# Rounding every second quad of an FFN's activations by a casting transfer instead of on VectorE

## The chip, the cores and the metric

The kernel runs on one core of a Trainium2 chip. The metric is the device time of one launch in microseconds (us); lower is better. The kernel before took 1745.02 us in the median of 3 runs (1744.55 to 1746.68).

The engines are written as the profile writes them: PE (TensorE, matrix products; PEld its weight loads), DVE (VectorE), ACT (ScalarE), POOL (GpSimd) and SP (SyncE, which issues the transfers of the kernel before).

## The reference

Four sequences of 12480 tokens with 128 channels go through an induced attention (32 learned points attend to the tokens, then the tokens attend to the result), and every token then through a feed-forward net with a squared ReLU.

```python
I = np.broadcast_to(inducing[None], (B, m, C))        # B, N, m, C = 4, 12480, 32, 128
def mab(q, kv):
    s = scale * (q @ kv.transpose(0, 2, 1))
    a = np.exp(s - s.max(-1, keepdims=True))
    a /= a.sum(-1, keepdims=True) + 1e-09
    return a @ kv
h = mab(I, x)
attn = mab(x, h)                                      # (4, 12480, 128)
h = np.maximum(attn.reshape(B * N, C) @ w_in, 0.0)    # w_in (128, 2048)
out = (h * h @ w_out)                                 # w_out (2048, 128)
```

## The kernel before

**Tiles.** The tokens are cut into 52 units of 960 tokens, 13 to a sequence (a batch). A unit has two blocks of 480 tokens. The 2048 hidden columns are 16 f-tiles of 128, and four f-tiles make a quad, so a block has four quads, j = 0 to 3.

**One quad.** PE forms h for four f-tiles (line 782), two to each of two PSUM tiles. ACT writes their ReLU into a tile g of 128 x 1920 (line 790, two instructions), then squares g in place (line 801). DVE writes hi, which is g rounded to the narrower format in which PE multiplies in one pass (line 805), and lo = g - hi (line 809). PE then adds twelve products to the block's output op in PSUM (line 822): hi with the high part of w_out, hi with its low part, and lo with its high part, four each. So each number of g is read by ACT, by DVE twice and by PE, and hi and lo are what PE waits for.

**The attention.** What the tokens' second attention gives a block (st) is made a unit ahead in small steps on PE, DVE and ACT (the class Second), with the eviction sw written by ACT or DVE, whichever the planner finds free (line 235), and four transfers sw to st. Beside it a first pass over a later unit runs (the class First): a load xn, a load xq that DVE turns into xt, scores, exponentials, and sums. After the last unit of a batch has had its first pass, a short stage joins the sums; GpSimd's instruction sums belongs to it. First passes run 14 units ahead, so the last units of the program have none beside them.

**What sets the order.** Nothing is ordered by hand. Each step is a task with an engine, a duration, a due time, the tasks it needs and the buffers it takes; the class Plan lays the tasks out in time, greedily, and the instructions are then written on each engine in the order of the plan's starts. LATENCY is what Plan adds between a task of an engine and one that needs it. An engine works its instructions in that order: one that waits holds up all behind it on its engine. GB, HB and LB are the numbers of buffers for g, hi and lo, and `room` tells Plan of them.

**Names.** In the order rows below a name such as hi_8_0_3 is followed by a running number: unit 8, block 0, quad 3 (the batch is left out). In h_8_1_5 the last figure is one of a block's eight PSUM tiles, two to a quad, so h_8_1_4 and h_8_1_5 feed g_8_1_2.

Of the kernel before, what the change touches and what calls it, by code (L numbers as in the profile page):

```python
# [12 lines left out]
F32R = mybir.dt.float32r  # L13
# [8 lines left out]
TS = 120  # L22
# [22 lines left out]
class Plan:  # L45
# [2 lines left out]

    ENGINES = ("PE", "ACT", "DVE", "POOL", "SP")

    LATENCY = {"PE": 220.0, "ACT": 150.0, "DVE": 185.0, "POOL": 150.0, "SP": 2500.0}
    SWITCH = 95.0
    LATE = {"PE": 200.0, "other": 100.0}

# [4 lines left out]
    def add(self, engine, ns, fn, due, needs=(), port=False, mode=None, takes=(), reads=(), late=None):  # L61

        if late is None:
            late = self.LATE["PE" if engine == "PE" else "other"] if due > self.begin else 0.0
        needs = [n for n in needs if n is not None]
        t = Task(engine.split("|"), ns, fn, due, needs, port, mode, takes, late, len(self.tasks))  # L70
        for b in list(takes) + list(reads):
            b.users.append(t)
        self.tasks.append(t)
        return t

    def run(self):
        free = {e: 0.0 for e in self.ENGINES}
        mode = None
        port = 0.0
        taken = {}  # L80
        open_ = {e: [] for e in self.ENGINES}
        done = []

        def offer(t):
            t.ready = 0.0
            for n in t.needs:
                own = n.by == "PE" and t.engine == ["PE"]
                t.ready = max(t.ready, n.end + (0.0 if own else self.LATENCY[n.by] + t.late))
            for e in t.engine:
# [24 lines left out]
        while len(done) < len(self.tasks):  # L114
            best = None
            for e in self.ENGINES:
                pick = None
# [37 lines left out]
def induced_attention_then_squared_relu_ffn(  # L155
# [8 lines left out]
    nc = tc.nc  # L164
    B, N, C = x.shape
    M = inducing.shape[0]
# [3 lines left out]
    NU = N // UNIT  # L170
    Q = P // M
    scale = 1.0 / math.sqrt(C)
    NQ = NF // 4
    GB, HB, LB = 3, 2, 2
    PERIOD, START, T_MAIN, NARROW, STEP = 32000.0, 2600.0, 66000.0, 6000.0, 1700.0
    W_DUE = [8000.0 + 6500.0 * k for k in range(8)]

# [3 lines left out]

    const = ctx.enter_context(tc.tile_pool(name="const", bufs=1))
    xn_pool = ctx.enter_context(tc.tile_pool(name="xn", bufs=3))
    xq_pool = ctx.enter_context(tc.tile_pool(name="xq", bufs=2))
    xt_pool = ctx.enter_context(tc.tile_pool(name="xt", bufs=NU + 1))
    hw_pool = ctx.enter_context(tc.tile_pool(name="hw", bufs=2))
    att = ctx.enter_context(tc.tile_pool(name="att", bufs=2))
# [1 line left out]
    ps_h = ctx.enter_context(tc.tile_pool(name="ps_h", bufs=2, space=PSUM))  # L189
    ps_o = ctx.enter_context(tc.tile_pool(name="ps_o", bufs=2, space=PSUM))  # L190
    ps_m = ctx.enter_context(tc.tile_pool(name="ps_m", bufs=2, space=PSUM))
    plan = Plan(dict(xn=3, early=6, xt=NU + 1, m=2, h=2, o=2, g=GB, hi=HB, lo=LB, st=2, sw=2, rows=2, xq=2, words=2), T_MAIN)

    def bank(name):
        return ps_m.tile([P, 512], F32, tag="m", name=name)
# [35 lines left out]
    add = plan.add  # L231
# [385 lines left out]
    class Second:  # L617
# [14 lines left out]
        def weigh(self, scored, where, bank_, due, step):  # L632
            v = {}
            n, s, u = self.n, self.s, self.u
# [37 lines left out]
                nc.vector.tensor_mul(v["d"], v["d"], v["rz"].broadcast_to([TS, G, M]))  # L672

            def high():
                v["sk"] = att.tile([TS, Q, 2, 2, M], F32R, tag="sk", name=f"sk_{n}")
                nc.vector.tensor_copy(v["sk"][:, :, :, 0, :], v["d"].rearrange("t (k q) m -> t q k m", q=Q))

            def low():
# [39 lines left out]
            t = add("DVE", 115, invert, d + 3 * step, [t])  # L718
            t = add("DVE", 340, share, d + 4 * step, [t], port=True)
            th = add("DVE", 210, high, d + 4 * step, [t], port=True)  # L720
            tl = add("DVE", 335, low, d + 5 * step, [th], port=True)
            t = add("PE", 460, back, d + 5 * step, [tl], takes=[ba])
# [38 lines left out]
    def ffn_block(b, u, k, second, t0, first_needs):  # L761
        n = f"{b}_{u}_{k}"
        s = state[b]
        w = {}
        bo = Buffer("o")
        part = PERIOD / 2 / NQ
        last = None

        def quad(j, last):
            v = {}  # L770
            due = t0 + j * part
            bg, bhi, blo = Buffer("g"), Buffer("hi"), Buffer("lo")
            relus = []
            for i in range(2):
                bh = Buffer("h")
                c = {}

                def wide(l, i=i, c=c):
                    if l == 0:
                        c["hp"] = ps_h.tile([P, 2, 512], F32, tag="h", name=f"h_{n}_{2 * j + i}")  # L780
                    f = 4 * j + 2 * i + l
                    nc.tensor.matmul(  # L782
                        c["hp"][:, l, :BLK], s["hw"][:, f * P:(f + 1) * P], s["st", u][:, k, :],
                        start=True, stop=True,
                    )

                def relu(i=i, c=c):
                    if i == 0:
                        v["g"] = pools["ffn"].tile([P, 4, BLK], F32, tag="g", name=f"g_{n}_{j}", bufs=GB)
                    nc.scalar.activation(v["g"][:, 2 * i:2 * i + 2, :], c["hp"][:, :, :BLK], AF.Relu)  # L790

                d = due + i * part / 2
                need = [second.ready, s["wide"][j]]
                t = add("PE", 219, lambda wide=wide: wide(0), d, need, takes=[bh], reads=[second.bst], late=LATE_G1)
                w.setdefault("begun", t)
                t = add("PE", 219, lambda wide=wide: wide(1), d, [t], reads=[bh, second.bst])
                relus.append(add("ACT", 864, relu, d + 1000, [t] + first_needs + relus, late=0,
                                 takes=[bg] if i == 0 else [], reads=[bh] + ([bg] if i else [])))

            def square():  # L800
                nc.scalar.activation(v["g"], v["g"], AF.Square)  # L801

            def high():
                v["hi"] = pools["ffn"].tile([P, 4, BLK], F32R, tag="hi", name=f"hi_{n}_{j}", bufs=HB)
                nc.vector.tensor_copy(v["hi"], v["g"])  # L805

            def low():
                v["lo"] = pools["ffn"].tile([P, 4, BLK], F32R, tag="lo", name=f"lo_{n}_{j}", bufs=LB)
                nc.vector.tensor_sub(v["lo"], v["g"], v["hi"])  # L809

            sq = add("ACT", 1706, square, due + 4000, relus, reads=[bg], late=0)
            th = add("DVE", 1070, high, due + 5700, [sq], port=True, late=200, takes=[bhi], reads=[bg])
            tl = add("DVE", 2070, low, due + 7800, [th], port=True, late=0, takes=[blo], reads=[bg, bhi])
            for m, (wo, name, from_, buf) in enumerate((
                (wo_hi, "hi", th, bhi), (wo_lo, "hi", th, bhi), (wo_hi, "lo", tl, blo),
            )):
                for i in range(2):
                    def products(i=i, wo=wo, name=name, m=m):
                        if j == m == i == 0:
                            w["op"] = ps_o.tile([P, 512], F32, tag="o", name=f"op_{n}")  # L820
                        for l in (2 * i, 2 * i + 1):
                            nc.tensor.matmul(  # L822
                                w["op"][:, :BLK], wo[:, 4 * j + l, :], v[name][:, l, :],
                                start=(j == m == l == 0), stop=(j == NQ - 1 and m == 2 and l == 3),
                            )

                    begin = j == m == i == 0
                    last = add("PE", 438, products, due + 8000 + 600 * (2 * m + i), [from_, last, w_outs[j]],
                               takes=[bo] if begin else [], reads=[buf] + ([] if begin else [bo]))
            return last  # L830

        for j in range(NQ):
            last = quad(j, last)

        def rows():
            w["rows"] = att.tile([P, BLK // M, M], F32, tag="rows", name=f"rows_{n}")
            nc.vector.transpose(w["rows"].rearrange("p g c -> p (g c)"), w["op"][:, :BLK])  # L837

        def store():
            for q in range(Q):  # L840
                nc.sync.dma_start(out_v[b, u, k, q], w["rows"][q * M:(q + 1) * M])

        br = Buffer("rows")
        end = t0 + PERIOD / 2 + 8000
        t = add("DVE", 570, rows, end + 1500, [last], reads=[bo], late=LATE_OT, takes=[br])
        add("SP", 2000, store, end + 4000, [t], reads=[br])
        return w["begun"]
# [19 lines left out]
    for w, (b, u) in enumerate(units):  # L867
# [4 lines left out]
        f = g = None  # L872
        if a < len(units):
            f = firsts[a] = First(*units[a], t_u + NARROW)
        if a - 1 < len(units):
            g = firsts[a - 1]
# [43 lines left out]
```

## Time and profile before

| | us |
|---|---|
| median of 3 runs | 1745.02 |
| the profiled execution's own time | 1748.76 |
| its span, first to last instruction | 1746.8 |
| PE busy in the span | 1687.7 |
| DVE busy | 1665.2 |
| ACT busy | 1588.2 |
| POOL busy | 25.8 |
| DVE's 416 casts to hi | 477.6 |
| DVE's 416 subtractions to lo | 896.0 |

Two more facts of the page: the clock granted to PE is at full speed from about 112 us on (mean 0.987 over the span), and the DMA engines are busy 31.7% of the time, nearly all of it with short packets.

How to read the rows that follow. In a row of groups stand line, engine, operation, the tile written and the tiles read, their shapes, the count, then busy us and mean ns of one, then the idle time of the engine just before such instructions and what ended it. In a row of the timeline stand start and length in us, engine, line and operation, with the count if several are merged; brackets give the idle time before it and its releaser. In a row of the chain stand start, length and what ran. Busy time of PE has modelled ends and counts pipelined matmuls longer than the distance at which they follow each other.

### The profile page before, as it was taken

How to read it: one execution, taken by the hardware profiler on the slowest of the kernel's cores; microseconds unless marked ns; L12 is line 12 of the kernel's file. 1: busy time of each engine (PE TensorE's matmuls, PEld its weight loads, DVE VectorE, ACT ScalarE, POOL GpSimd, SP SyncE). 2: the span in 40 equal slices, each digit the busy share in tenths (PEclk: the TensorE clock that was granted, in tenths of full speed). 3: DMA queues.
4: the chain of work that ended last, by engine and by line, in shares of the span. 5: the costliest groups of instructions: out<-in, count | busy, mean ns of one | idle time of the engine just before them, and what ended most of it. 6: DMA issues, size and time to landing. Idle time of an engine off the chain costs nothing.

```text
span 1746.8 us, 23651 instructions
## 1 busy us (share of the span) xinstructions
PE 1687.7 (97%) x8897; PEld 1339.3 (77%) x8897; DVE 1665.2 (95%) x1777; ACT 1588.2 (91%) x1581; POOL 25.8 (1%) x22
## 2 busy tenths in 40 slices
PE   7699999999999999999999999999999999999998
PEld 4378777777877777777777877777787888888886
DVE  5689999999999999999999999999999999999998
ACT  5399999999989999999998999999998999999997
POOL 1200000000000000000000000000000000000000
PEclk9699999999999999999999999999999999999999
DMA  9742342333333333333423333423211121211111
GB/s 207 128 68 47 63 74 53 62 68 63 61 59 57 60 66 63 63 57 63 73 47 63 64 56 63 74 47 62 40 29 35 29 40 29 41 29 37 32 27 30
DMA packets 428781, 101.61 MB, mean 58 GB/s; under 512 B 362844, under 2 KB 428156, under 8 KB 428668
## 3 DMA queue, kind: packets, MB, share of 16 engines
q1 hardware_dynamic: 428668, 100.11, 31.7%
q8 instruction: 70, 1.15, 0.3%
q14 instruction: 43, 0.35, 0.1%
HBM read 48.94 MB, written 25.56 MB: 43 GB/s over the span
## 4 chain that ended last, share of the span: by engine, by line
PE 51%; DVE 30%; issue 11%; ACT 6%; DMA 2%; SPq 0%; DVEq 0%; POOL 0%; ACTq 0%
PE op L822 35%; PE h L782 12%; DVE lo L809 10%; DVE hi L805 10%; ACT g L801 3%; ACT g L790 2%; DVE rows L837 2%; DVE xt L401 1%; PE na L626 1%; DMA xn<-in_x_dram 1%; DVE sw L235 1%; DVE d L672 1%; DVE sk L680 1%; PE wp L586 1%; DMA words_o<-in_moe_w_out_dram 1%
## 5 line engine op out<-in xcount | busy, mean ns | idle before, releaser
L809 DVE TENSOR_TENSOR lo<-g,hi 128x1920 fp32r<-128x1920 f32 x416 | 896.0, 2154 | 16.2 <-PE na L430 0.5
L790 ACT ACTIVATE g<-h 128x960 f32<-128x960 f32 x832 | 783.0, 967 | 96.1 <-PE h L782 82.6
L801 ACT ACTIVATE g<-g 128x1920 f32<-128x1920 f32 x416 | 752.9, 1810 | 8.2
L782 PE MATMUL h<-st,hw 128*128 128x480 f32 x1664 | 517.9, 389 | 12.7 <-ACT g L790 8.2
L805 DVE CAST hi<-g 128x1920 fp32r<-128x1920 f32 x416 | 477.6, 1148 | 25.1 <-ACT g L801 19.7
L822 PE MATMUL op<-lo,wo_hi 128*128 128x480 f32 x1664 | 459.3, 390 | 15.2 <-DVE lo L809 15.1
L822 PE MATMUL op<-hi,wo_hi 128*128 128x480 f32 x1664 | 462.6, 386 | 1.3 <-DVE hi L805 1.0
L822 PE MATMUL op<-hi,wo_lo 128*128 128x480 f32 x1664 | 432.3, 382 | 0.0
L782 PEld LDWEIGHTS h<-st,hw 128*128 128x128 f32 x1664 | 308.7, 189 | 104.3 <-ACT g L790 54.3
L822 PEld LDWEIGHTS op<-lo,wo_hi 128*128 128x128 f32 x1664 | 297.4, 189 | 87.5 <-DVE lo L809 42.0
L822 PEld LDWEIGHTS op<-hi,wo_hi 128*128 128x128 f32 x1664 | 304.1, 188 | 68.7 <-DVE hi L805 20.2
L822 PEld LDWEIGHTS op<-hi,wo_lo 128*128 128x128 f32 x1664 | 313.8, 189 | 49.9
L837 DVE STREAM_TRANSPOSE rows<-op 128x480 f32<-128x480 f32 x104 | 70.4, 677 | 1.3 <-PE op L822 1.2
L401 DVE STREAM_TRANSPOSE xt<-xq 128x960 f32<-128x960 f32 x39 | 45.7, 1172 | 4.3 <-PE na L626 4.3
L687 PEld LDWEIGHTS ap<-identr,sk 120*128 120x128 f32 x208 | 31.4, 193 | 7.3 <-issue 4.0
L626 PE MATMUL na<-xt,hT 128*32 128x240 f32 x416 | 32.7, 387 | 0.0
L687 PE MATMUL ap<-identr,sk 120*128 120x120 f32 x208 | 29.5, 265 | 2.5 <-DVE sk L680 2.5
L235 ACT COPY xt<-xtp 128x480 f32<-128x480 f32 x26 | 14.3, 559 | 16.4 <-PE xtp L415 16.4
L564 POOL TENSOR_SCALAR sums<-ones,zs 128x128 f32<-128x128 f32 x4 | 8.8, 2209 | 1228.1 <-PE lp L548 800.0
L464 PE MATMUL ep<-ident,e 128*120 128x128 f32 x104 | 21.5, 290 | 5.0 <-ACT e L456 3.3
L415 PE MATMUL xtp<-ident,xn 120*128 120x120 f32 x104 | 18.6, 319 | 7.6 <-DMA xn<-in_x_dram 7.6
L430 PE MATMUL na<-xt,indT 128*32 128x240 f32 x312 | 23.8, 378 | 0.9 <-DVE xt L401 0.9
(90 smaller groups left out, 616.6 us busy)
## 6 DMA issues: line engine op xcount, KB each, us to landing
xn<-in_x_dram SPq DMA_DIRECT2D x52, 480.0 KB, 4.9
st<-sw SPq DMA_DIRECT2D x208, 120.0 KB, 2.3
out_dram<-rows SPq DMA_DIRECT2D x416, 60.0 KB, 2.0
xq<-in_x_dram SPq DMA_DIRECT2D x156, 120.0 KB, 3.6
words_i<-in_moe_w_in_dram SPq DMA_DIRECT2D x4, 512.0 KB, 10.2
words_o<-in_moe_w_out_dram SPq DMA_DIRECT2D x4, 512.0 KB, 9.2
ind_sb<-in_inducing_dram SPq DMA_DIRECT2D x1, 16.0 KB, 1.6
```

Source lines behind the costliest of these rows:

```text
L235: ENG[task.by](dst, src)
L401: nc.vector.transpose(self.xt, v["xq"].rearrange("p g c -> p (g c)"))
L430: nc.tensor.matmul(where[q * M:(q + 1) * M, :], indT, self.xt[:, q * 2 * TS:(q + 1) * 2 * TS], start=True, stop=True,)
L626: nc.tensor.matmul(where[q * M:(q + 1) * M, :].rearrange("m (k t) -> m k t", k=2), self.s["hT"][:, :M], self.s["xt"][self.u].rearrange("c ...
L687: nc.tensor.matmul(ap[:, q * TS:(q + 1) * TS], v["sk"][:, q].rearrange("t k a m -> t (k a m)"), identr[:TS, :TS], start=(q == 0), stop=(q ...
L782: nc.tensor.matmul(c["hp"][:, l, :BLK], s["hw"][:, f * P:(f + 1) * P], s["st", u][:, k, :], start=True, stop=True,)
L790: nc.scalar.activation(v["g"][:, 2 * i:2 * i + 2, :], c["hp"][:, :, :BLK], AF.Relu)
L801: nc.scalar.activation(v["g"], v["g"], AF.Square)
L805: nc.vector.tensor_copy(v["hi"], v["g"])
L809: nc.vector.tensor_sub(v["lo"], v["g"], v["hi"])
L822: nc.tensor.matmul(w["op"][:, :BLK], wo[:, 4 * j + l, :], v[name][:, l, :], start=(j == m == l == 0), stop=(j == NQ - 1 and m == 2 and l = ...
L837: nc.vector.transpose(w["rows"].rearrange("p g c -> p (g c)"), w["op"][:, :BLK])
```

## The change

In quads 1 and 3 of each block the task that writes hi is put on a new planner engine, CAST. Its instruction is a transfer issued by GpSimd from g to hi, both in SBUF, 128 x 1920 numbers of 4 bytes (960 KB), which casts to hi's format on the way. Quads 0 and 2 keep the cast on DVE. lo stays on DVE in all quads, and now waits for the transfer in the odd ones. There are 4 such transfers in a unit, 208 in all.

The planner's table gives CAST a latency of 4500 beside the task's 1070, and the odd quads' task no longer claims the port that DVE shares with GpSimd in the planner's rules. g gets four buffers instead of three and hi three instead of two; xq, and sk of the second attention, go from two to one, which makes the room.

```diff
-    ENGINES = ("PE", "ACT", "DVE", "POOL", "SP")
-
-    LATENCY = {"PE": 220.0, "ACT": 150.0, "DVE": 185.0, "POOL": 150.0, "SP": 2500.0}
+    ENGINES = ("PE", "ACT", "DVE", "POOL", "SP", "CAST")
+
+    LATENCY = {"PE": 220.0, "ACT": 150.0, "DVE": 185.0, "POOL": 150.0, "SP": 2500.0, "CAST": 4500.0}
...
-    GB, HB, LB = 3, 2, 2
+    GB, HB, LB = 4, 3, 2
...
-    xq_pool = ctx.enter_context(tc.tile_pool(name="xq", bufs=2))
+    xq_pool = ctx.enter_context(tc.tile_pool(name="xq", bufs=1))
...
-    plan = Plan(dict(xn=3, early=6, xt=NU + 1, m=2, h=2, o=2, g=GB, hi=HB, lo=LB, st=2, sw=2, rows=2, xq=2, words=2), T_MAIN)
+    plan = Plan(dict(xn=3, early=6, xt=NU + 1, m=2, h=2, o=2, g=GB, hi=HB, lo=LB, st=2, sw=2, rows=2, xq=1, words=2), T_MAIN)
...
-                v["sk"] = att.tile([TS, Q, 2, 2, M], F32R, tag="sk", name=f"sk_{n}")
+                v["sk"] = att.tile([TS, Q, 2, 2, M], F32R, tag="sk", name=f"sk_{n}", bufs=1)
...
                 v["hi"] = pools["ffn"].tile([P, 4, BLK], F32R, tag="hi", name=f"hi_{n}_{j}", bufs=HB)
-                nc.vector.tensor_copy(v["hi"], v["g"])
+                if th.by == "CAST":
+                    nc.gpsimd.dma_start(v["hi"], v["g"])
+                else:
+                    nc.vector.tensor_copy(v["hi"], v["g"])
...
-            th = add("DVE", 1070, high, due + 5700, [sq], port=True, late=200, takes=[bhi], reads=[bg])
+            th = add("CAST" if j % 2 else "DVE", 1070, high, due + 5700, [sq], port=not j % 2, late=200, takes=[bhi], reads=[bg])
```

Since Plan sets the order, most rows on PE, DVE and ACT move. Three places in the steady stage of the first batch show how.

**First place: from hi of quad 3 in block 0 of unit 8 on.** PE before:

```order
L822 MATMUL op_8_0_3398<-hi_8_0_3_3511,wo_hi 128x480 x4
L822 MATMUL op_8_0_3398<-hi_8_0_3_3511,wo_lo 128x480 x4
L782 MATMUL h_8_1_3_3526<-st_8_3304,hw_883 128x480
L822 MATMUL op_8_0_3398<-lo_8_0_3_3524,wo_hi 128x480 x4
L782 MATMUL h_8_1_4_3547<-st_8_3304,hw_883 128x480 x2
L782 MATMUL h_8_1_5_3555<-st_8_3304,hw_883 128x480
L822 MATMUL op_8_1_3557<-hi_8_1_0_3540,wo_hi 128x480 x4
```

PE with the change, up to the first product of the next unit:

```order
L825 MATMUL op_8_0_3417<-hi_8_0_3_3516,wo_hi 128x480 x4
L825 MATMUL op_8_0_3417<-hi_8_0_3_3516,wo_lo 128x480 x4
L825 MATMUL op_8_1_3548<-hi_8_1_0_3540,wo_lo 128x480 x4
L782 MATMUL h_8_1_5_3572<-st_8_3199,hw_880 128x480 x2
L825 MATMUL op_8_1_3548<-lo_8_1_0_3546,wo_hi 128x480 x2
L825 MATMUL op_8_0_3417<-lo_8_0_3_3562,wo_hi 128x480 x4
L825 MATMUL op_8_1_3548<-lo_8_1_0_3546,wo_hi 128x480 x2
L782 MATMUL h_8_1_6_3585<-st_8_3199,hw_880 128x480 x2
L782 MATMUL h_8_1_7_3590<-st_8_3199,hw_880 128x480 x2
L782 MATMUL h_9_0_0_3602<-st_9_3497,hw_880 128x480 x2
```

hi of quad 3 now stands behind the first products of the next block, and h_8_1_4 (not shown) two rows ahead of it. Between its start and the end of h_8_1_5 are 14 matmuls. DVE in the same stretch, before:

```order
L837 STREAM_TRANSPOSE rows_8_0_3570<-op_8_0_3398 128x480
L805 CAST hi_8_1_1_3580<-g_8_1_1_3534 128x1920
L235 CAST sw_9_3592<-ap_9_3575 128x480
L809 TENSOR_TENSOR lo_8_1_1_3598<-g_8_1_1_3534,hi_8_1_1_3580 128x1920
L805 CAST hi_8_1_2_3615<-g_8_1_2_3564 128x1920
L809 TENSOR_TENSOR lo_8_1_2_3622<-g_8_1_2_3564,hi_8_1_2_3615 128x1920
```

and DVE with the change, where the last row reads the hi that a transfer wrote:

```order
L812 TENSOR_TENSOR lo_8_0_3_3562<-g_8_0_3_3474,hi_8_0_3_3516 128x1920
L840 STREAM_TRANSPOSE rows_8_0_3587<-op_8_0_3417 128x480
L808 CAST hi_8_1_2_3599<-g_8_1_2_3551 128x1920
L812 TENSOR_TENSOR lo_8_1_2_3623<-g_8_1_2_3551,hi_8_1_2_3599 128x1920
L812 TENSOR_TENSOR lo_8_1_1_3634<-g_8_1_1_3538,hi_8_1_1_3570 128x1920
```

The cast of quad 1 is gone, and lo of quad 1 has moved behind cast and lo of quad 2.

**Second place: PE from hi of quad 1 in block 1 of unit 8 on,** before:

```order
L822 MATMUL op_8_1_3557<-hi_8_1_1_3580,wo_hi 128x480 x4
L822 MATMUL op_8_1_3557<-hi_8_1_1_3580,wo_lo 128x480 x4
L782 MATMUL h_8_1_7_3594<-st_8_3304,hw_883 128x480
L822 MATMUL op_8_1_3557<-lo_8_1_1_3598,wo_hi 128x480 x4
L822 MATMUL op_8_1_3557<-hi_8_1_2_3615,wo_hi 128x480 x4
L782 MATMUL h_9_0_0_3628<-st_9_3602,hw_883 128x480 x2
L822 MATMUL op_8_1_3557<-hi_8_1_2_3615,wo_lo 128x480 x4
L782 MATMUL h_9_0_1_3639<-st_9_3602,hw_883 128x480 x2
L822 MATMUL op_8_1_3557<-lo_8_1_2_3622,wo_hi 128x480 x4
```

and with the change (s2t belongs to the second attention):

```order
L825 MATMUL op_8_1_3548<-hi_8_1_1_3570,wo_hi 128x480 x4
L825 MATMUL op_8_1_3548<-hi_8_1_1_3570,wo_lo 128x480 x4
L782 MATMUL h_9_0_1_3642<-st_9_3497,hw_880 128x480 x2
L782 MATMUL h_9_0_2_3645<-st_9_3497,hw_880 128x480 x2
L825 MATMUL op_8_1_3548<-lo_8_1_1_3634,wo_hi 128x480 x4
L825 MATMUL op_8_1_3548<-hi_8_1_2_3599,wo_hi 128x480 x4
L825 MATMUL op_8_1_3548<-hi_8_1_2_3599,wo_lo 128x480 x4
L825 MATMUL op_8_1_3548<-lo_8_1_2_3623,wo_hi 128x480 x4
L782 MATMUL h_9_0_3_3692<-st_9_3497,hw_880 128x480 x2
L644 MATMUL s2t_10_3695<-ident,ss_10_3651 120x128 x2
L782 MATMUL h_9_0_4_3698<-st_9_3497,hw_880 128x480 x2
```

hi of quad 1 now follows the first h of the next unit. From its start to the end of h_9_0_3 are 30 matmuls of 480 columns, 18 of them from lo_8_1_1 on. ACT at that place, with the change:

```order
L801 ACTIVATE g_8_1_3_3597<-g_8_1_3_3597 128x1920
L790 ACTIVATE g_9_0_0_3625<-h_9_0_1_3642 128x960
L790 ACTIVATE g_9_0_1_3659<-h_9_0_2_3645 128x960
L801 ACTIVATE g_9_0_0_3625<-g_9_0_0_3625 128x1920
L456 ACTIVATE e_1_10_3684,z_10_3683<-na_10_3605,neg_10_3655 128x240
L459 ACTIVATE fade_10_3686<-neg_9_3357,neg_10_3655 128x1
L790 ACTIVATE g_9_0_1_3659<-h_9_0_3_3692 128x960
L790 ACTIVATE g_9_0_2_3708<-h_9_0_4_3698 128x960
L801 ACTIVATE g_9_0_1_3659<-g_9_0_1_3659 128x1920
```

Before, each square followed the two ReLUs of its own quad; now the ReLU of the next quad's first tile stands ahead of it (h_9_0_4 ahead of the square of g_9_0_1).

**Third place: PE from hi of quad 1 in block 0 of unit 9 on,** with the change:

```order
L825 MATMUL op_9_0_3715<-hi_9_0_1_3733,wo_hi 128x480 x4
L825 MATMUL op_9_0_3715<-hi_9_0_1_3733,wo_lo 128x480 x4
L782 MATMUL h_9_1_0_3800<-st_9_3497,hw_880 128x480 x2
L782 MATMUL h_9_1_1_3803<-st_9_3497,hw_880 128x480 x2
L825 MATMUL op_9_0_3715<-lo_9_0_1_3784,wo_hi 128x480 x4
L825 MATMUL op_9_0_3715<-hi_9_0_2_3774,wo_hi 128x480 x4
L825 MATMUL op_9_0_3715<-hi_9_0_2_3774,wo_lo 128x480 x4
L825 MATMUL op_9_0_3715<-lo_9_0_2_3805,wo_hi 128x480 x4
L782 MATMUL h_9_1_2_3830<-st_9_3497,hw_880 128x480 x2
L782 MATMUL h_9_1_3_3833<-st_9_3497,hw_880 128x480 x2
L782 MATMUL h_9_1_4_3841<-st_9_3497,hw_880 128x480 x2
L825 MATMUL op_9_1_3846<-hi_9_1_0_3838,wo_hi 128x480 x4
```

The next row is hi_9_0_3, so that 38 matmuls lie from hi_9_0_1 to it, and 30 from hi_9_0_1 to the end of h_9_1_2. At the same place before:

```order
L822 MATMUL op_9_0_3696<-hi_9_0_1_3729,wo_hi 128x480 x2
L782 MATMUL h_9_0_6_3756<-st_9_3602,hw_883 128x480 x2
L822 MATMUL op_9_0_3696<-hi_9_0_1_3729,wo_hi 128x480 x2
L822 MATMUL op_9_0_3696<-hi_9_0_1_3729,wo_lo 128x480 x4
L782 MATMUL h_9_0_7_3774<-st_9_3602,hw_883 128x480 x2
L782 MATMUL h_9_1_0_3780<-st_9_3602,hw_883 128x480
L822 MATMUL op_9_0_3696<-lo_9_0_1_3764,wo_hi 128x480 x4
L782 MATMUL h_9_1_0_3780<-st_9_3602,hw_883 128x480
L782 MATMUL h_9_1_1_3793<-st_9_3602,hw_883 128x480 x2
L822 MATMUL op_9_0_3696<-hi_9_0_2_3782,wo_hi 128x480 x4
L822 MATMUL op_9_0_3696<-hi_9_0_2_3782,wo_lo 128x480 x4
L782 MATMUL h_9_1_2_3812<-st_9_3602,hw_883 128x480
```

There hi of quad 3 came before the next block's first products, and h of the later tiles was spread between them. On POOL the 208 transfers follow one another, with the three later sums instructions between them; SP's list keeps its instructions.

## The prediction

> **What bounds the kernel now.** I read the page's engine shares first, then the chain of waits in order of time, then the busy time by stretch.
>
> ```profile
> PE 1687.7 (97%) x8897; PEld 1339.3 (77%) x8897; DVE 1665.2 (95%) x1777; ACT 1588.2 (91%) x1581; POOL 25.8 (1%) x22
> 370.01 2.21 PE op L822 x8
> 402.02 2.22 PE op L822 x8
> 434.07 2.20 PE op L822 x8
> 599.47 2.21 PE op L822 x8
> ...
> 1419.13 2.63 PE op L822 x12
> 1479.09 2.62 PE op L822 x12
> 304.00:400.00 96.00, 94.25 (x506) 75.68 (x505) 94.41 (x100) 90.13 (x88) 0.00 (x0) 1.00 0.34 62
> 1420.00:1540.00 120.00, 119.51 (x571) 97.85 (x570) 116.97 (x109) 116.11 (x105) 0.00 (x0) 1.00 0.18 34
> ```
>
> In the chain (start, length) the same piece returns every 32.0 us: that is one unit (two blocks of four quads). A batch change (434 to 599, five units) costs 5.4 us more. Late in the program, where no first pass of a later unit runs along, two units take 59.96 us, 29.98 each. The stretches (length, then PE, weight loads, DVE, ACT, POOL, clock, DMA share, GB/s) show 94.41 of 96 us busy on DVE, 31.5 per unit of 32.0, at full clock. ACT has 30.0, and PE's busy time counts modelled ends. So in the main stage (about 112 to 1360 us, 38 units after three batch changes) DVE is the fullest engine, with PE close; in the tail (12.5 units) PE is, at 119.51 of 120.
>
> **What is taken away.** Groups by line:
>
> ```profile
> L809 DVE TENSOR_TENSOR lo<-g,hi 128x1920 fp32r<-128x1920 f32 x416 | 896.0, 2154 | 16.2 <-PE na L430 0.5
> L790 ACT ACTIVATE g<-h 128x960 f32<-128x960 f32 x832 | 783.0, 967 | 96.1 <-PE h L782 82.6
> L805 DVE CAST hi<-g 128x1920 fp32r<-128x1920 f32 x416 | 477.6, 1148 | 25.1 <-ACT g L801 19.7
> L235 DVE CAST sw<-ap 128x480 fp32r<-128x480 f32 x34 | 22.1, 650 | 0.0
> L235 ACT CAST sw<-ap 128x480 fp32r<-128x480 f32 x18 | 9.9, 548 | 0.9 <-PE ap L687 0.9
> ```
>
> Four of eight casts per unit leave DVE: 4 x 1.148 = 4.6 us. The new order also gives 39 instead of 18 of the 52 sw evictions to ACT: 21 x 0.65 / 52 = 0.3 us less on DVE, 0.2 us more on ACT. DVE falls to 31.5 - 4.9 = 26.6 us per unit and stops being a bound; ACT stands at 30.2. If nothing else changed, a unit could shrink by somewhat less than 1.8 us.
>
> **What is added: a latency in a loop.** In place of 1.15 us on DVE, an odd quad's rounded part now takes L: from the end of ACT's square over the issue on GpSimd, the movement of 960 KB from SBUF to SBUF and its landing, to PE's first matmul on hi. PE runs its matmuls in a fixed order, so L is hidden only as far as other work stands between; the order rows shown with the change give that work. The steps' durations come from the timeline of before:
>
> ```profile
> 401.88 1.16 DVE L805 CAST hi<-g 128x1920 fp32r<-128x1920 f32 x1
> 403.14 2.16 DVE L809 TENSOR_TENSOR lo<-g,hi 128x1920 fp32r<-128x1920 f32 x1
> 404.08 0.59 PE L782 MATMUL h<-st,hw 128*128 128x480 f32 x2
> 404.70 0.97 ACT L790 ACTIVATE g<-h 128x960 f32<-128x960 f32 x1 [0.20 <-PE h L782]
> 407.01 1.81 ACT L801 ACTIVATE g<-g 128x1920 f32<-128x1920 f32 x1
> 407.56 0.60 PE L822 MATMUL op<-hi,wo_hi 128*128 128x480 f32 x2
> 408.00 1.04 PE L822 MATMUL op<-hi,wo_lo 128*128 128x480 f32 x4
> 408.86 1.16 DVE L805 CAST hi<-g 128x1920 fp32r<-128x1920 f32 x1 [0.23 <-ACT g L801]
> 408.88 0.59 PE L782 MATMUL h<-st,hw 128*128 128x480 f32 x2
> 426.21 0.98 ACT L790 ACTIVATE g<-h 128x960 f32<-128x960 f32 x1 [0.29 <-PE h L782]
> 427.22 1.81 ACT L801 ACTIVATE g<-g 128x1920 f32<-128x1920 f32 x1
> 427.25 2.16 DVE L809 TENSOR_TENSOR lo<-g,hi 128x1920 fp32r<-128x1920 f32 x1
> 428.94 1.81 ACT L790 ACTIVATE g<-h 128x960 f32<-128x960 f32 x2
> 429.32 0.42 DVE L680 TENSOR_TENSOR sk<-d,sk 120x256 fp32r<-120x256 f32 x1
> 430.78 1.81 ACT L801 ACTIVATE g<-g 128x1920 f32<-128x1920 f32 x1
> ```
>
> From these: a 480-column matmul 0.22 us (407.56 to 408.88, six); last h matmul to relu 0.18 (404.08 + 0.44 to 404.70); relu to a square 1.01, two relus 1.84, a square 1.81; square to DVE 0.04; cast to its lo 1.26, lo to the next DVE instruction 2.07. For lo's end to PE I take 0.06, an estimate near the 0.04 of the other hop.
>
> Loop one, once around per unit. PE starts on hi_8_0_3 (unit 8, block 0, quad 3): 14 matmuls until h_8_1_5 is done, 3.08; hop 0.18; relu 1.01; square 1.81; DVE's cast of quad 2 0.04 + 1.26; lo of quad 2 2.07; lo of quad 1, queued behind it, 2.16 + 0.06: 11.67. PE waits there for lo_8_1_1; from it 18 matmuls to h_9_0_3, 3.96; hop 0.18; two relus 1.84; square of g_9_0_1 1.81: 19.46. Then L, and from hi_9_0_1 another 38 matmuls to hi_9_0_3, 8.36. The unit cannot be shorter than 27.8 + L.
>
> Loop two, with two transfers: hi_8_1_1 to h_9_0_3 is 30 matmuls, 6.60 + 0.18 + 1.84 + 1.81 = 10.43, then L; hi_9_0_1 to h_9_1_2 is 30 more, 6.60 + 0.18, three relus 2.76, square 1.81 = 11.35, then L. That makes 21.8 + 2L, the longer one above L = 6.0.
>
> Against 32.0 us the point of balance is **L = 4.2 us**.
>
> **The size of L.** The trace shows no transfer from GpSimd and none that casts. The nearest rows (KB each, us from issue to landing; then the rates in 40 slices of 2 to 12 us, where the DMA engines were full):
>
> ```profile
> xn<-in_x_dram SPq DMA_DIRECT2D x52, 480.0 KB, 4.9
> st<-sw SPq DMA_DIRECT2D x208, 120.0 KB, 2.3
> ind_sb<-in_inducing_dram SPq DMA_DIRECT2D x1, 16.0 KB, 1.6
> GB/s 2 51 152 49 82 268 328 319 209 238 209 297 254 147 279 360 377 371 279 299 223 170 166 156 207 217 203 168 162 182 217 201 190 176 197 197 201 197 180 207
> DMA packets 3239, 2.10 MB, mean 210 GB/s; under 512 B 62, under 2 KB 3108, under 8 KB 3239
> ```
>
> The smallest lands in 1.6 us. The other 944 KB (967 thousand bytes) take 2.6 us at the best slice, 377 GB/s, and 4.6 at the mean of 210: L = 4.2 to 6.2. Carried on from xn (3.3 us for 464 KB more) it is 1.6 + 6.7 = 8.3, the upper end. xn goes in pieces of 512 bytes; here each partition is one run of 7680 bytes over all 128 partitions, so I lean to the fast slices: 300 GB/s, 3.2 us, 4.8 in all. GpSimd writes the transfer's descriptors itself and other transfers hold the DMA engines 34% of the time; I add 0.6 (an estimate), and take **L = 5.4**.
>
> By the Trainium skill (DMA: Bandwidth & Descriptors, Anatomy of one DMA) a GpSimd transfer costs about 2.0 us fixed and its bytes at 436 GB/s. That would be 4.25 us (an estimate from the page) and a unit of 32.05; no row here moves at 436.
>
> **The sum.** Main stage: 27.8 + 5.4 = 33.2, +1.2 x 38 units = +46. Tail: its order has a shorter loop of the first kind in every second unit (one relu and ten matmuls fewer on the path, 3 us), so between 30.2 and 33.2; I take 31.0, nearer the shorter, since the longer comes only every second unit, +1.0 x 12.5 = +13. The profiled execution took 1748.76 with a span of 1746.8, 3.7 above the median of 1745.0; +59 makes it 1808, and the median 1804.
>
> **What costs nothing.** The single sk buffer is rewritten a unit after PE read it. With one xq buffer the load waits on SP for the turn of the unit before; what stands behind it in SP's queue is due half a unit later, and xq lands in 3.6 us. If that cover went, each late xq would cost at most those 3.6 us on DVE, which has 5 us of room. The g and hi buffers cost only room. DMA moves 3.9 MB more per unit, 118 GB/s on top of 62: under the 210 shown, yet st may land later; its reader is half a unit away. Three sums instructions stand between transfers in POOL's queue, 2.2 us each in the page: 7 us at most, left to the range.
>
> **Rivals.**
> - *DVE's relief wins.* The loops overcount (durations overlap at their ends) and L is below 4. Then ACT's 30.2 and PE set the pace; halfway to 32.0, 31.1: -0.9 x 38 = -34, tail unchanged: 1711. For it: DVE's 31.5. Against: no row carries 960 KB that fast. It decides below L = 4.2.
> - *It just fits.* L = 4.2, tail 29.98: 1745. This is what the page's 4.25 us would give.
> - *GpSimd waits for DVE.* Per element, CAST takes 0.6 ns and the two-input lo 1.12, so CAST moves two at a time. If the writing of descriptors must wait for whichever is running, the mean wait is (8 x 2.154² + 4 x 1.148²) / (2 x 33) = 0.64 us: L = 6.05, unit 33.9, +72, tail +19: 1836. The Trainium skill (SBUF — State Buffer, Who interferes with whom) has this lock for a two-port copy or cast, which starves descriptors, and only infers that a two-input instruction does not. By its rule for casts alone the mean is 0.08 us, and nothing changes.
> - *The casting transfer is slow.* At xn's pace L is near 7.5: 21.8 + 15 = 36.8, +182; tail 33.5, +44: 1971. Against: xn's short pieces.
>
> **Chances.** Forecast (L 4.4 to 6) 0.51; relief 0.17; just fits 0.08; lock 0.12; slow transfer 0.12. The forecast and the last two are slower: 0.75. A difference under 0.2%, 3.5 us, is no change here. The forecast's own range is 1755 to 1835; the range to hold 8 in 10, 1725 to 1910, takes in part of the relief and leaves out the slow transfer.
>
> **What would show it.** Right: the DMA issues part lists hi<-g from POOL, 208 of 960 KB, landing in about 5 us; PE waits at op on hi and lo of odd quads, put down to the DMA or to DVE's lo; DVE near 27 us per unit; pieces of the chain 33 us apart. Wrong: a landing under 4 us; a unit of 31 with ACT or PE as the releaser; or landings far above 6 with units longer than 21.8 + 2L.

## The result and the profile after

The changed kernel takes **1915.5 us** (median of 4 runs, 1910.1 to 1920.0) against 1745.4 for the kernel before: 1.097 times as long, 95% interval 1.094 to 1.101. The forecast was 1804, with a range of 1725 to 1910. The direction was right; 170 us were lost where 59 had been worked out.

Of the page of the changed kernel: the engines' shares, the chain by engine, the casting transfers among the DMA issues (count, size, median us to landing), and the groups that answer to those shown of before.

```profile
PE 1710.5 (90%) x8897; PEld 1342.1 (70%) x8897; DVE 1462.8 (77%) x1548; ACT 1590.1 (83%) x1602; POOL 128.9 (7%) x230
PE 37%; ACT 21%; issue 15%; DVE 14%; DMA 11%; SPq 2%; DVEq 0%; ACTq 0%; POOLq 0%; POOL 0%
L790 ACT ACTIVATE g<-h 128x960 f32<-128x960 f32 x832 | 769.5, 970 | 178.1 <-PE h L782 171.3
L808 DVE CAST hi<-g 128x1920 fp32r<-128x1920 f32 x208 | 240.8, 1158 | 227.5 <-ACT g L801 226.1
hi<-g POOLq DMA_DIRECT2D x208, 960.0 KB, 4.1
```

DVE is relieved as planned (1665 to 1463 us), and the transfers land sooner than forecast, in 4.1 us. Yet no engine is full any more: ACT stands idle in front of its ReLUs for 178 us, where it was 96, and DVE in front of its casts for 228, where it was 25. Who waits for whom, in the changed kernel (us in total, times, longest):

```profile
ACT g L790 <- PE h L782: 171.3, 172, 2.9
PEld h L782 <- ACT g L790: 159.0, 180, 2.6
PE h L782 <- ACT g L790: 100.0, 119, 2.2
PEld op L825 <- DMA hi<-g: 41.7, 43, 3.7
DVE lo L812 <- DMA hi<-g: 28.8, 28, 3.4
PE op L825 <- DMA hi<-g: 25.3, 34, 3.4
```

and the same view of the kernel before:

```profile
ACT g L790 <- PE h L782: 82.6, 191, 3.3
PEld h L782 <- ACT g L790: 54.3, 149, 1.0
PE h L782 <- ACT g L790: 8.2, 39, 0.6
```

The waits for the transfer are the smaller part: 25 us on PE and 42 on its weight loads, which overlap, and 29 on DVE. (The chain puts 6% of the span, some 115 us, down to the transfers, but a share of the chain is not what would be saved without them.) What grew between PE and ACT is a pair: ACT's ReLU waits for h, +89 us, and PE's h waits for ACT's ReLU, +92. The h matmul reads only st and hw, so what it waits for in a ReLU can only be its PSUM tile: ACT must empty one of the two before PE may write the next. The chain of waits in the tail (start, length, what) shows the two engines taking turns, in the changed kernel:

```profile
1658.65 4.59 PE op L825 x20
...
1678.51 3.52 PE op L825 x16
1682.03 0.44 PE h L782 x2
...
1682.49 0.98 ACT g L790
...
1683.52 0.71 PE h L782 x2
1684.23 3.51 PE op L825 x16
...
1708.37 1.73 ACT g L790 x2
...
1726.15 4.59 PE op L825 x20
```

and in the kernel before, where PE alone carries the chain:

```profile
1431.57 0.43 PE h L782 x2
1432.00 0.88 PE op L822 x4
1432.88 0.44 PE h L782 x2
1433.32 1.76 PE op L822 x8
```

Before, mostly 2 to 8 products of op stand between two h's. Now 16 to 20 often stand together, and the pairs of h stand close behind one another. Counted over PE's instructions from 112 to 1300 us, 66% of the products stand in runs of 16 or more, against 3% before. While PE works off a long run (1684 to 1688), ACT gets no new h, and stands idle for 1.27 us before its next ReLU; where the pairs of h are bunched, PE waits until ACT has emptied a tile, and ACT alone carries the chain (around 1710). No transfer stands in the chain of these two units, which take 67.5 us, against 59.96 before.

### The profile page after: what moved, and what is told of

It reads as the page before. It is cut to its first block, busy times and chain, and to the rows that moved or that the text cites. A ratio compares the mean times of both kernels' runs of the same rounds, so it can differ in the third digit from the quotient of the medians.

```text
span 1908.3 us, 24030 instructions
## 1 busy us (share of the span) xinstructions
PE 1710.5 (90%) x8897; PEld 1342.1 (70%) x8897; DVE 1462.8 (77%) x1548; ACT 1590.1 (83%) x1602; POOL 128.9 (7%) x230
## 4 chain that ended last, share of the span: by engine, by line
PE 37%; ACT 21%; issue 15%; DVE 14%; DMA 11%; SPq 2%; DVEq 0%; ACTq 0%; POOLq 0%; POOL 0%
PE op L825 27%; ACT g L790 12%; DVE lo L812 7%; ACT g L801 7%; PE h L782 7%; DMA hi<-g 6%; DVE hi L808 3%; DMA xq<-in_x_dram 3%; SPq L397 1%; DMA words_i<-in_moe_w_in_dram 1%; DVE xt L401 1%; PE wp L586 1%; PE na L626 1%; DVE d L655 1%; ACT d L658 1%
## 5 line engine op out<-in xcount | busy, mean ns | idle before, releaser
L790 ACT ACTIVATE g<-h 128x960 f32<-128x960 f32 x832 | 769.5, 970 | 178.1 <-PE h L782 171.3
L812 DVE TENSOR_TENSOR lo<-g,hi 128x1920 fp32r<-128x1920 f32 x416 | 882.4, 2153 | 36.9 <-DMA hi<-g 28.8
L782 PE MATMUL h<-st,hw 128*128 128x480 f32 x1664 | 481.7, 393 | 104.3 <-ACT g L790 100.0
L825 PE MATMUL op<-lo,wo_hi 128*128 128x480 f32 x1664 | 429.5, 385 | 17.9 <-DVE lo L812 17.5
L808 DVE CAST hi<-g 128x1920 fp32r<-128x1920 f32 x208 | 240.8, 1158 | 227.5 <-ACT g L801 226.1
L806 POOL DMA_DIRECT2D hi<-g x208 | 110.6, 532 | 1701.6 <-ACT g L801 1366.3
L840 DVE STREAM_TRANSPOSE rows<-op 128x480 f32<-128x480 f32 x104 | 70.7, 679 | 82.6 <-PE op L825 82.6
L658 ACT ACTIVATE d<-d 120x256 f32<-120x256 f32 x52 | 21.7, 417 | 55.4 <-DVE d L655 55.4
L651 DVE TENSOR_REDUCE mx<-s2t 120x8 f32<-120x256 f32 x52 | 21.8, 419 | 20.2 <-PE s2t L644 20.0
L662 DVE TENSOR_REDUCE z<-d 120x8 f32<-120x256 f32 x52 | 20.8, 401 | 17.0 <-ACT d L658 17.0
L235 ACT COPY et<-ep 120x256 f32<-120x256 f32 x52 | 19.4, 374 | 16.7 <-PE ep L464 16.0
```

The source lines that it names most:

```text
L658: nc.scalar.activation(v["d"], v["d"], AF.Exp, scale=scale)
L782: nc.tensor.matmul(c["hp"][:, l, :BLK], s["hw"][:, f * P:(f + 1) * P], s["st", u][:, k, :], start=True, stop=True,)
L806: nc.gpsimd.dma_start(v["hi"], v["g"])
L825: nc.tensor.matmul(w["op"][:, :BLK], wo[:, 4 * j + l, :], v[name][:, l, :], start=(j == m == l == 0), stop=(j == NQ - 1 and m == 2 and l = ...
```

## The experiments

Two theories stood against each other. **Order**: the planner, told that the new task takes 4.5 us until it can be used, lays the work out in another order, and that order is slow by itself. **Latency**: as predicted, the transfer is a delay in a loop. A third, **buffers**, was that the single xq and sk cost something after all.

### The buffers alone

```diff
-            th = add("CAST" if j % 2 else "DVE", 1070, high, due + 5700, [sq], port=not j % 2, ...)
+            th = add("DVE", 1070, high, due + 5700, [sq], port=True, ...)
```

> The buffers of the change (g 4, hi 3, xq 1, sk 1) with all casts on DVE, so the planner lays out an order of its own for them, without transfers. Theory 'order' (the changed order of PE, ACT and DVE sets the time of the changed kernel, not the transfer): about as before, 1735 to 1755 us, a unit of 32.0. Theory 'latency' (the transfer's latency in the loops of the record): the same. Theory 'buffers' (the single xq or sk buffer makes loads or narrow steps late): above 1800.

Measured: 1742.9 us, ratio 0.998 (0.997 to 0.999). The buffers cost nothing.

### The order without its transfers

```diff
-                if th.by == "CAST":
+                if False:
```

> The changed kernel's order on every engine, laid out as if the transfer existed, but the odd quads' hi is written by a DVE cast that stands in DVE's list at the place that the plan gave the transfer; no transfer runs. Latency from the square to hi falls from about 4.5 us to 1.2 us where DVE is free. Theory 'order': still far above before, 1860 to 1940 us, with ACT and PE waiting on one another. Theory 'latency': the loops fall to about 29 us, DVE (31.5 us per unit) becomes the bound again, and the time is 1740 to 1770 us.

Measured: 1922.9 us, ratio 1.101 (1.099 to 1.104): as slow as with the transfers, and with the same pair of waits:

```profile
ACT g L790 <- PE h L782: 168.8, 164, 2.8
PE h L782 <- ACT g L790: 114.0, 144, 2.1
```

DVE has its casts back here, so its load could stand in for what the transfers cost. The run with hi free, below, takes that away.

### The transfers in the order of before

```diff
-                if th.by == "CAST":
+                if j % 2:
...
-            th = add("CAST" if j % 2 else "DVE", 1070, high, ...)
+            th = add("DVE", 1070, high, ...)
```

> The planner lays out all casts on DVE (as in e1), but the odd quads' cast is then issued as the transfer from GpSimd. Nothing in the order makes room for it. An odd quad's hi comes some 3 us later than its place (0.3 + 4.1 against 1.2), four times per unit. Theory 'latency': a full 13 us per unit is lost less the slack of the order, a unit of 38 to 45 us, 2050 to 2400 us. Theory 'order': a stall too, but less than in the changed kernel per us of latency if PE and ACT keep alternating: 1900 to 2100 us.

Measured: 2310.5 us, ratio 1.323 (1.321 to 1.326).

```profile
DVE lo L812 <- DMA hi<-g: 526.4, 169, 7.9
PE op L825 <- DMA hi<-g: 398.2, 191, 5.1
```

So latency is no phantom: in an order that does not provide for it, a 4.2 us landing costs 565 us. A part of that may be the clock, 0.93 granted here; it wasn't separated. The planner's 4.5 us bought that off, at a price.

### One number of the planner: products due later

Plan takes, of the tasks that can start within 40 ns, the one due first (`key = (0.0 if start <= free[e] + 40.0 else start, t.due, t.order)`). A quad is 4 us of the planned unit, and its products are due 8 to 11 us behind its start. With the transfer's latency those of an odd quad become ready only after that, so they are overdue, and go in one run ahead of the h matmuls of quads that start later. Due at 14 us, they no longer do.

```diff
-                    last = add("PE", 438, products, due + 8000 + 600 * (2 * m + i), ...)
+                    last = add("PE", 438, products, due + 14000 + 600 * (2 * m + i), ...)
```

> The changed kernel, all 208 transfers and buffers as they are, with one number changed: the output products' due time is 14000 instead of 8000 after the quad's, so that the planner lets the h matmuls go ahead of late products. Theory 'order': the runs of h matmuls that wait for ACT go, and the time falls under that of before: a unit of 30.5 to 32 us, 1680 to 1745 us. Theory 'latency': the transfers are as long as before and the loops through them stay near 27.8 + 4.5 = 32.3 us and above: 1770 to 1920 us.

Measured: 1737.0 us, ratio 0.995 (0.994 to 0.997), with all 208 transfers. The pair of waits is down:

```profile
ACT g L790 <- PE h L782: 77.6, 118, 6.7
PE h L782 <- DMA st<-sw: 25.6, 30, 3.7
PE h L782 <- ACT g L790: 11.7, 17, 2.1
```

and a wait for st, made of four short transfers, is the new row. Of the products, 2% are left in runs of 16 or more.

### The order with nothing in the place of the transfers

```diff
+                if th.by == "CAST" and "hc" in pools:
+                    v["hi"] = pools["hc"]
+                    return
...
+                    pools["hc"] = v["hi"]
```

> The changed kernel's order, with nothing at all in the place of the 208 transfers but the first: hi of quads 1 and 3 is one tile, filled once, so that 207 roundings are left out and VectorE's 208 others stay (VectorE keeps the relief, 26 to 27 us per unit). Theory order (the planner's new order strands ScalarE behind TensorE's two PSUM tiles of h): the waits on hi<-g go, 25 us on PE and 29 us on DVE, but the wait of ACT's ReLU for h stays at 150 us or more, and the time at 1870 to 1915. Rival latency (the loops of the prediction with L = 0, 27.8 and 21.8 us, so TensorE's own 30.4 us per unit bounds): 1700 to 1750, and the wait of the ReLU for h falls to some 80 us.

Measured: 1878.7 us, ratio 1.076 (1.074 to 1.078). DVE has the relief, hi of the odd quads is there from the start (it is filled once, so that 207 roundings are left out), and still 133 of the 170 us are lost: they are the order's. The pair of waits is as it was with the transfers, and so are the runs (66% of the products in runs of 16 or more):

```profile
ACT g L790 <- PE h L782: 160.2, 166, 2.9
PE h L782 <- ACT g L790: 102.5, 127, 2.0
```

The chain shows its period in the main stage, 34.4 us against 32.0, and in the tail, 67.5 for two units, as with the transfers:

```profile
654.29 3.74 PE op L829 x16
...
658.50 0.98 ACT g L790
...
660.23 3.52 PE op L829 x16
...
683.54 1.81 ACT g L801
...
685.38 1.16 DVE hi L812
686.54 2.08 DVE lo L816
...
688.66 3.79 PE op L829 x16
...
1561.29 4.53 PE op L829 x20
...
1628.76 4.53 PE op L829 x20
```

(2.4 x 38 + 3.75 x 12.5 = 138, against 133 measured. Some units of the tail are shorter than these two: by the ends of the units in both traces the main stage, batch changes included, lost 91 us and the tail 38.) The transfers add 37 to that.

### Each transfer twice

```diff
                     nc.gpsimd.dma_start(v["hi"], v["g"])
+                    nc.gpsimd.dma_start(v["hi"], v["g"])
```

> The changed kernel with every casting transfer issued a second time into the same tile, so that hi of the odd quads is there some 4.1 us later. The prediction's loops (21.8 + 2L in loop two, L from 4.5 to 8.6): 39.0 us per unit against the 34.6 seen, 1915 + 50 x 4.4 = 2135. Theory order (most transfers have slack where they stand, and a few are waited for, 34 waits of PE and 28 of DVE, which become more): less than one extra microsecond per unit and microsecond, 1950 to 2080.

Measured: 2537.7 us, ratio 1.452 (1.447 to 1.458), far above both. The second transfer waits in GpSimd for the first, with 4.7 us each, so hi comes 0.53 + 4.7 = 5.2 us later, not 4.1:

```profile
POOL hi L807 <- DMA hi<-g: 892.6, 191, 9.4
L806 POOL DMA_DIRECT2D hi<-g x208 | 110.8, 533 | 1222.7 <-ACT g L801 1131.4
L826 PE MATMUL op<-hi,wo_hi 128*128 128x480 f32 x1664 | 538.3, 447 | 455.5 <-DMA hi<-g 452.7
```

622 us over 50.5 units and 5.2 us are 2.4 us per unit for each us of lateness: beyond what the plan provides for, the slope is near the 2L of the predicted loop two; that it is this loop isn't shown. A part of it is the clock, 0.88 granted here against 0.986, with a matmul of this group at 447 ns against 392; that part wasn't separated. Order's "less than 1" was wrong, and so was the predicted loop's 2135 us.

### The same number in the kernel before

The edit is the one above, 14000 in place of 8000, in the kernel before.

> The kernel before, with no transfer and no buffer changed, and the products of a quad due 14 us behind its start in the planner's table where it was 8. It says how much of what the same number gave the changed kernel (1915 to 1737) is the number's own. Theory order (the number undoes what the 4.5 us of latency did to the order): the kernel before has no such damage, its wait of the ReLU for h is 83 us already, so 1725 to 1750. Rival (the number is worth 170 us to any order): below 1700.

Measured: 1698.2 us, ratio 0.973 (0.971 to 0.974). Order's expectation was too high, and the rival's "below 1700" came in, though with 47 us and not 170. The kernel before was losing time to its order, too: its ReLU's wait for h falls from 82.6 to

```profile
ACT g L790 <- PE h L782: 30.3, 37, 6.9
```

so 47 us of what the number gave the changed kernel are to be had without any transfer. They are not all shown to be that wait's: the new order also gives 23 of the 34 sw evictions on DVE to ACT, which takes 15 us off DVE.

### The transfer planned at 3.3 us

```diff
-    LATENCY = {..., "CAST": 4500.0}
+    LATENCY = {..., "CAST": 3300.0}
```

(on top of products due at 14 us.)

> The changed kernel with products due at 14 us and the transfer's latency 3300 ns in the planner's table in place of 4500 (its landing was measured at 4.1). Theory order: lo and the products are put 1.2 us earlier, closer to what the transfer takes, 1710 to 1740 if the landing still fits, as at 4500. Rival latency (a transfer planned shorter than it is, is waited for each time): some 1 us more in two of four quads, 1790 to 1840.

Measured: 1746.9 us, ratio 1.001 (1.000 to 1.003), between the two expectations: lo's wait for the transfer is 115 us in place of 25. With the 1.07 us of the task itself the table now has 4.4 us, and the transfers land in 4.7 in this run. Planning it shorter than it lands has a cost, but here a small one.

### The mended order without transfers

The edit that frees hi, with products due at 14 us.

> The order of the run with products due at 14 us, to the instruction, with nothing in the place of its transfers but the first (hi of quads 1 and 3 is one tile, filled once; 207 roundings left out). What stays between this and 1737 is what the transfers themselves cost in an order that suits them: their lateness and what they do to other transfers (st<-sw lands in 3.4 us there, in 2.3 where no casting transfer runs). Theory order (the transfers fit, as planned 4.5 us against 4.5 landed): 1725 to 1740. Rival (transfers are the rest of the loss, by landing late now and then and by crowding st<-sw, both of which the chain there shows with 5% and 7%): 1690 to 1710, and st<-sw back at 2.3 us.

Measured: 1694.5 us, ratio 0.971 (0.969 to 0.973), as the rival had it: the transfers cost 42.5 us in this order. st lands in

```profile
st<-sw SPq DMA_DIRECT2D x208, 120.0 KB, 2.3
```

against 3.4 us with them.

### Only the odd quads' products due later

```diff
-                    last = add("PE", 438, products, due + 8000 + 600 * (2 * m + i), ...)
+                    last = add("PE", 438, products, due + (14000 if j % 2 else 8000) + 600 * (2 * m + i), ...)
```

> The changed kernel with the later due time, 14 us, for the products of the transferred quads 1 and 3 alone; quads 0 and 2 keep 8. If what spoils the order is that products of late quads come up overdue and are then put ahead of the h matmuls, whichever quad they belong to: part of the loss goes, 1760 to 1850 (the products of all quads of a block are one sequence, so those of quad 2 stand behind those of quad 1 and come up overdue still). If it is those of the transferred quads alone: 1735 to 1750, as with all four. If the due time is not what counts: 1900 to 1920.

Measured: 1784.4 us, ratio 1.022 (1.020 to 1.024): 131 of the 179 us that all four gave, a ReLU's wait for h of 145 us, between 171 and 78, and 35% of the products in runs of 16 or more, between 66 and 2. It isn't the transferred quads alone.

### Later still, with and without transfers

Products due at 16 us, the transfer planned at 5000 ns:

> The changed kernel, products due at 16 us and the transfer planned at 5000 ns: a search for an order in which the 208 transfers cost nothing. If lateness is what stays (8 of 100 landings take 6 us and more), half a microsecond of margin takes off some waits: 1715 to 1735. If what stays is the crowding of st<-sw, it does not: 1737 and above.

Measured: 1727.7 us, ratio 0.990 (0.986 to 0.993). That lies in the range for lateness, but two numbers were changed at once, and lo's wait for the transfer hardly moved (23.4 us against 24.7), so the 9 us are not shown to be the margin's. And the kernel before with products due at 16 us:

> The kernel before with products due at 16 us, no transfer: whether 14 us is the end of what the number gives there (1698). TensorE is busy 1653 us of 1696 with it, so no more than some 10 us can be left: 1690 to 1705.

Measured: **1691.7 us**, ratio 0.969 (0.968 to 0.971), the fastest of all. PE is busy 98% of the span, and its line leads the chain with 87%:

```profile
PE 1648.0 (98%) x8897; PEld 1349.5 (80%) x8897; DVE 1634.8 (97%) x1752; ACT 1577.0 (93%) x1606; POOL 22.0 (1%) x22
```

### Transfers that nobody waits for

```diff
+                    v["hi"] = wo_hi.rearrange("p f c -> p (f c)")[:, :4 * BLK].rearrange("p (l t) -> p l t", l=4)
+                    idle = pools["ffn"].tile([P, 4, BLK], F32R, tag="idle", ..., bufs=1)
+                    nc.gpsimd.dma_start(idle, v["g"])
+                    return
```

hi of the odd quads is then a part of wo_hi that is there from the start, and their rounding is left out. In the changed kernel's order:

> The changed kernel's order with all 208 casting transfers issued where they were, but into a tile that nobody reads; hi of quads 1 and 3 is a view of wo_hi (their rounding is left out of the result). Nobody waits for a transfer's data; what stays is its traffic beside the other transfers, and g held until it has landed. Without any transfer this order takes 1878.7, with them 1915.5. If the 37 us are the lateness of hi: 1875 to 1885. If they are the traffic: 1905 to 1920.

and in that with products due at 14 us:

> The same with products due at 14 us: 1694.5 without any transfer, 1737.0 with them. If what stays is the lateness of hi (lo waits 25 us for it, PEld 6 us): 1694 to 1705, and st<-sw lands in 3.4 us all the same without cost. If it is the traffic, which lands st<-sw, the h matmuls' moving operand, 1.1 us later (26 us of TensorE's waits there): 1720 to 1740.

Measured: 1876.1 us (ratio 1.075, 1.073 to 1.077) and 1731.3 (0.992, 0.990 to 0.994). The two orders pay for the transfers in different ways:

| us | changed order | products due at 14 us |
|---|---|---|
| the order, no transfer | 1878.7 | 1694.5 |
| transfers beside it, nobody waits | 1876.1 (-2.6, within the intervals) | 1731.3 (+36.8) |
| transfers, hi used | 1915.5 (+39.4) | 1737.0 (+5.7) |

In the changed order the transfers' traffic is free and their lateness costs 39 us. In the mended order lateness costs 6 us and the traffic 37: the landing of st, median, and what PE waits for it, with transfers that nobody reads (against 2.3 us and a wait of 3.6 us without transfers):

```profile
st<-sw SPq DMA_DIRECT2D x208, 120.0 KB, 3.7
PE h L782 <- DMA st<-sw: 26.8, 28, 3.6
```

That wait is 23 us longer, of the 37; g is also held until its transfer has landed, and the rest wasn't separated.

## Why the prediction was wrong

**What bounds the kernel.** Right for the main stage and the tail as they stood. Missed was that the kernel before was already losing time to the order: one number of the planner takes it to 1691.7.

**What is taken away.** Right. Of the changed kernel, two pieces of the chain a unit apart, and two stretches (length, PE, weight loads, DVE, ACT, POOL, clock, DMA share, GB/s):

```profile
704.72 3.73 PE op L825 x16
739.45 3.79 PE op L825 x16
588.00:657.00 69.00, 62.52 (x332) 49.83 (x332) 53.87 (x56) 59.30 (x59) 4.24 (x8) 1.00 0.66 170
1590.55:1726.15 135.60, 123.30 (x570) 97.28 (x569) 102.59 (x95) 115.80 (x103) 8.48 (x16) 1.00 0.46 146
```

A unit of the main stage takes 34.7 us, of which DVE works 53.87 x 34.7 / 69 = 27.1, as forecast; in the tail four units hold 102.59, 25.6 each. But the relief is worth next to nothing once the order is mended: with it and without any transfer 1694.5, without it 1698.2 with the same due time and 1691.7 with 16 us.

**The size of L.** Too large. A landing of 4.1 us, counted from the start of GpSimd's issue, and 0.29 from the square's end to that start (both medians) make about 4.4, not 5.4. An estimate from the Trainium skill (DMA: Bandwidth & Descriptors, Anatomy of one DMA: 2.0 us and the bytes at 436 GB/s) is 4.25; the trace agrees within 0.2. Had the sum been right otherwise, with L = 4.4 a unit would then have taken 32.2 us and the kernel some 1753 (0.2 x 38 more, the tail as before), further off than the forecast.

**The sum: the step that failed.** "The unit cannot be shorter than 27.8 + L" is a lower bound from two loops through hi, and was taken for the time of the unit. The loops count each h and each ReLU once, at its duration. They leave out the other loop of the same order: h waits for one of two PSUM tiles, the tile for its ReLU, the ReLU for ACT, which stands idle while PE works off 16 products and is then asked for three tiles at once. That loop has no L in it. In the chain of one unit with hi free it comes twice (behind 16 products an h, its ReLU, and the h that waits for it, from 658 and from 664 us on), and the way of an even quad's ReLU, square, cast and lo (682 to 689) closes the round. The two predicted loops give at most 27.8 us with L = 0; measured are 34.4 per unit with hi free, above even the 33.2 predicted with L = 5.4, and 33.7 in the two units of the tail against 31.0. The order rows shown ahead of the prediction have it already: two or three pairs of h, then 16 products, where before an h stood behind every 4 or 8. That is how it could have been seen. That the two PSUM tiles are the link rests on the waits and on what h reads; no run with a third tile was made.

**Main stage and tail.** Forecast +46 and +13. With hi free, by the ends of the units, the order costs 91 and 38. The transfers add 37, some 4 of them in the tail, whose two units take 67.5 us with and without them.

**What costs nothing.** Buffers: right, 1742.9. DMA traffic: right in this order (-2.6), and wrong as a rule: +37 in the other. "st may land later; its reader is half a unit away" was the sentence that fails there.

**Rivals.** Relief: refuted by the runs with hi free. It just fits: the landing did, the time didn't. GpSimd waits for DVE: refuted for lo, which was most of its price. Of the 208 issues of the changed kernel 199 stand beside a lo, and they take 0.53 us in the median and 0.58 at most; none stands beside a cast. For the cast the wait is real. In the run with the transfer planned at 3.3 us 57 issues meet a cast on DVE, and 48 of them end 0.12 us behind the cast's end, the longest after 1.50 us. One of them (start, length):

```profile
257.45 1.15 DVE L808 CAST hi<-g 128x1920 fp32r<-128x1920 f32 x1
257.47 1.25 POOL L806 DMA_DIRECT2D hi<-g  x1 [8.43 <-DVE lo L812]
```

The Trainium skill (SBUF — State Buffer, Who interferes with whom) has it so: a cast can hold up GpSimd's writing of descriptors, and a two-input instruction, as it infers, does not. The traces agree with both.

Slow casting transfer: refuted by the landing of 4.1 us. None of the rivals was an order that is slow by itself. Where the planner lays out everything anew, that one is needed.

## What to carry to other kernels

If a change moves a planner's latency, price the new order apart from the operation: put nothing in the operation's place and run the order alone. A loop through the new operation is only a lower bound; look in the changed order for every pair of engines that hand few buffers back and forth, and count what stands between two uses. Taking work off a nearly full engine gained nothing here, where the engine beside it was just as full, and a better order was worth more than the relief.

## What was not expected of the hardware

- GpSimd's transfer of 960 KB from SBUF to SBUF with a cast lands in 3.9 us at best, 4.1 in the median and 8.4 at most in the changed kernel, and costs GpSimd 0.53 us. That is 240 GB/s including all fixed time, for 4.1 us. It depends on what else is in flight: 4.0 us in the median for the 31 with no other transfer beside them, 6.1 for the 35 beside an xn of 480 KB.
- Beside such transfers, short ones land later: the pieces of 120 KB for st in 3.4 us (products due at 14 us) and 3.7 (there with nobody waiting) where they took 2.3. In the changed order, with as many transfers, the median stays at 2.3 us because fewer pieces meet one. Those issued from 1 us before a transfer's issue to 2 us behind it are 76 of 208 there, and land in 4.3 us; with products due at 14 us they are 126, and land in 4.7; the others take 2.3 and 2.4. (In the run with only the odd quads' products later, 73 such pieces land in 2.6, so it isn't the distance alone.)
- With PE busy 75% and 80% of the span, in waits of several us, the granted clock was 0.88 (each transfer twice) and 0.93 (transfers in the order of before); in the other traces it was 0.98 to 0.99. Whether the waits are its cause wasn't tried.
